# Hash attention and MLP on one core: the preparation of the first batch, and the order of the third chunk, written anew

## The chip, the core and the metric

The kernel runs on one core of a Trainium2 chip. The metric is the device time of one execution in microseconds (us). The kernel before was timed in three runs: 324.23, 325.96 and 326.18 us, median 325.96. All times below are from one profiled execution, counted from its first instruction.

## What is computed

```python
q_bits = (np.einsum('bhsd,dk->bhsk', q, proj) > 0)      # k_bits likewise; 6 bits
mask = q_bucket[:, :, :, None] == k_bucket[:, :, None, :]
scores = np.where(mask, scale * np.matmul(q, k.transpose(0, 1, 3, 2)), -1e9)
attn = softmax(scores); x = attn @ v                    # (4, 8, 768, 64)
# x as (4, 768, 512):
xn = (x - mu) / np.sqrt(var + 1e-06) * g_ln
out = x + np.maximum(xn @ w_ch1, 0.0) @ w_ch2           # 512 -> 2048 -> 512
```

There are 4 batches of 8 heads, with 768 tokens of 64 elements. A key counts for a query only when all six signs of their projections agree.

## The kernel before

**Trick of the mask.** The kernel puts the six sign bits beside the 64 elements of each query and key, as plus or minus one half or a multiple of it. One matmul over 70 rows then gives the score plus a large amount for equal bits; a bias in the exponential takes that amount off again, so that unequal hashes vanish. The operands stand in `slots`: rows 0 to 63 are the elements, rows 64 to 69 the bits, for each head, for queries and keys, with 768 columns in two halves (`par` 0 and 1).

**Chunks and units.** A chunk is 256 queries of one batch (`TT` = 2 tiles of 128), so each batch has three chunks, 12 in all. A chunk has 12 units (`att_units`, L385): three for each of four pairs of heads. A unit is 4 score matmuls (L403) into a tile `sc` in PSUM, one exponential on ScalarE (`ex`, L409, 128 x 1024) and 8 matmuls with the values (`av`, L437). At the third unit of a pair VectorE divides by the row sums (L452, L462). The first group of a pair needs head a alone; the second needs both heads. Behind attention comes the MLP of the chunk (`mlp_steps`, L470): norm, `xtrans`, eight `up` steps (8 matmuls L519 each, evacuated by `evac`, L125, to `hbuf`) and eight `down` steps (4 matmuls L536 each), which are spread as fillers between the units of the next chunk by `interleave` (L598) according to a cost written beside each step.

**Preparation of batch 0** is done by TensorE, since nothing else has run yet. For each head, `transposes` (L202) turns q and k with three transposes each into a PSUM tile `tpose` (VectorE evacuates q, L219, ScalarE k, L221, to `qkT` in f32), and `casts` (L223) writes `qkT` as bf16 into `slots`, one cast for each half. For each pair, `hash_pair` (L299) projects q (a = 0) and k (a = 1) with 4 matmuls each (L306), VectorE makes bits of them (L311), and four copies (L326, L324 or L322) of 6 x 768 put the bits into `slots`: two or three on VectorE, one on GpSimd, one on ScalarE for the first pair. `values` (L328) casts half of v for the matmuls with the values, `row_sums` (L349) prepares the row `vrows` with which every `av` begins in batch 0.

**The first two chunks** are one stage, `first_two` (L644), in an order written by hand (`tc.manual_schedule()`: each engine takes its instructions in the order of the program). The units go pair by pair, and the third chunk's first scores are the last of the list. In round i the scores of the next unit are issued, then the steps of `also[i]`, then the values of unit i. `keep_awake` issues matmuls on zeros. Loads: q, k and v of batch 0 on SP's queue (k of the first two heads and proj on ScalarE's), w1, w2 and batch 1 on GpSimd's.

**Preparation of batches 1 to 3** is named by letters in `plan` (L708): L load of q and k, W load of v, N narrowing cast on GpSimd (L239), T the DMA transpose into `slots` (L261) and the copy of half of it (L266), K and B block transposes on VectorE (L244), H hashes on TensorE (L275) with a way over DRAM for the bits (L288, L290), V cast and sums of values, E their share (L344), Q the squares on ScalarE (L191) for a safety test. These are fillers too. From the third chunk on, a scheduler may move instructions; it works with costs of its own.

**Buffers that matter:** `ps_sc`, `ps_av` and `ps_mm` have two tiles each; `tpose` (but for head 1), hashes, `rows`, `xnTp`, `hp` and `o2` share `ps_mm`. `qkT` has four, `nat16` one, `ex` three.

Of the kernel before, what the change touches and what calls it, by code (L numbers as in the profile page):

```python
# [28 lines left out]
def kernel(  # L29
# [12 lines left out]
    P = 128  # L42
# [115 lines left out]
    def load_values(b, half):  # L158
        h0 = half * H // 2
        eng = nc.gpsimd if (b, half) == (1, 0) else nc.sync  # L160
        if (b, half) == (0, 1):
# [6 lines left out]
        eng.dma_start(  # L168
            out=t, in_=v[b, h0 : h0 + H // 2].rearrange("h (p c) d -> p h c d", p=P)
        )  # L170
        return t

    class Prep:
# [28 lines left out]
        def transposes(self, h, a):  # L202
# [3 lines left out]
            if h == 1:  # L206
                tp = ps_sc.tile([P, 2, 512], F32, tag="sc", name="tpose")[:, 0, 0:HS]
# [10 lines left out]
            if a == 0:  # L218
                nc.vector.tensor_scalar_mul(self.qkT[h][:, a, :], tp, Q_SCALE)  # L219
            else:  # L220
                nc.scalar.activation(self.qkT[h][:, a, :], tp, AF.Copy)  # L221

        def casts(self, h):  # L223
            src = self.qkT[h]
            if h < 2:
                nc.gpsimd.tensor_copy(self.tokens(h, 0), src[0:D])
                nc.scalar.activation(self.tokens(h, 1), src[D:P], AF.Copy)
            else:
                eng = nc.gpsimd if h in (4, 6) else nc.vector
                eng.tensor_copy(self.tokens(h, 0), src[0:D])  # L230
                nc.vector.tensor_copy(self.tokens(h, 1), src[D:P])  # L231
# [67 lines left out]
        def hash_pair(self, j, a):  # L299
# [15 lines left out]
            if a == 0:  # L315
                return
            for g in range(4):
                par = g % 2
                dst = self.sl[D:K1, 2 * j + g // 2, :, par * HS : (par + 1) * HS]
                src = bits[32 * g : 32 * g + n_bits]  # L320
                if g == 2 and j == 0:
                    nc.scalar.activation(dst, src, AF.Copy)  # L322
                elif g == 3:
                    nc.gpsimd.tensor_copy(dst, src)  # L324
                else:
                    nc.vector.tensor_copy(dst, src)  # L326
# [143 lines left out]
    def mlp_steps(b, t, x):  # L470
# [41 lines left out]
        def up(n2):  # L512
# [3 lines left out]
            for i in range(2):  # L516
# [11 lines left out]
                scalar=b == 0 and t == 0 and n2 < NH // 2 - 2,  # L528
# [110 lines left out]
    def head(h):  # L639
        prep.transposes(h, 0)  # L640
        prep.transposes(h, 1)
        prep.casts(h)

    def first_two():  # L644
# [20 lines left out]
        keep_awake(10)  # L665
        prep.values(0)
# [5 lines left out]
            0: [lambda: head(2), lambda: prep.values(1)],  # L672
            1: [lambda: prep.row_sums(0), lambda: head(3), lambda: nxt.load(0)],
            3: [lambda: prep.hash_pair(1, 0)],
            4: [lambda: prep.hash_pair(1, 1)],
            5: [lambda: head(4), load_w2],
            6: [lambda: head(5)],
            7: [lambda: prep.hash_pair(2, 0)],
            8: [
                lambda: prep.row_sums(1), lambda: prep.hash_pair(2, 1), lambda: nxt.load(1), lambda: nxt.load_v(0),  # L680
            ],
            9: [lambda: head(6)],
            10: [lambda: head(7)],
            11: [lambda: prep.hash_pair(3, 0)],
            12: [
                lambda: prep.hash_pair(3, 1), lambda: nxt.narrow(0, 0), lambda: nxt.narrow(0, 1),
            ],
            14: [lambda: nxt.blocks(0, 0, 0)],
            15: [
                lambda: nxt.blocks(0, 0, 1),  # L690
            ],
# [12 lines left out]

# [31 lines left out]
    for n in range(2, len(chunks)):  # L736
# [4 lines left out]
        fillers = (mlp[0][1][1:] if n == 2 else []) + [norm]  # L741
        fillers += mixed(early, tail[:4]) + ([(600, xtrans)] if n == 2 else [])
        held = ups[-2:] if n == len(chunks) - 1 else []
        fillers += mixed(late, tail[4:]) + ups[: len(ups) - len(held)]
# [8 lines left out]
        interleave(units[n], fillers, after, begun=True)  # L753
# [190 lines left out]
```

## Time and profile before

| what | value |
|---|---|
| three runs | 324.23, 325.96, 326.18 us; median 325.96 us |
| profiled execution | span 325.2 us from first to last instruction; a time of its own around that span is not given |
| TensorE matmul busy | 305.4 us (94%), 3249 instructions |
| ScalarE, VectorE, GpSimd busy | 216.8, 181.4, 83.8 us |
| exponentials | 144 of 1114 ns, 159.7 us |
| up matmuls, down matmuls | 99.0 us, 92.4 us |
| first exponential; first of the third chunk | 11.99 us; 52.06 us |

A matmul's busy time is partly modelled, so that a busy TensorE is not one at its peak. "Granted clock" (PEclk) is the share of the TensorE clock that its throttle let through. In tables of waits, an engine and line stand ahead of the arrow and what ended the wait behind it, then total, times, and the longest, in us. Lines of the timeline have the start, the length, engine, line, operation, output <- input, and in brackets the idle time before it and what ended it.

### The profile page before, as it was taken

Reading aid. Unit: us, or ns where it says so; the run is one execution under the profiler, and the core shown is the slowest. Engines: PE = TensorE matmul, PEld = TensorE weight load, DVE = VectorE, ACT = ScalarE, POOL = GpSimd, SP = SyncE. Lnnn points to the kernel's source line nnn. Section 1 sums busy time; section 2 is a strip of 40 time slices with the busy share of each in tenths; the row PEclk is TensorE's granted clock in tenths of the full one; section 3 lists DMA queues with packets and bytes.
Section 4 is the critical chain, followed back from the end, with each engine's and each line's share of the span. In section 5 each row is a group of like instructions: output and inputs, shape, how many; then the busy total and the mean of one; then the engine's idle time right before and its main releaser. Section 6 shows DMA issues by size and latency. Waiting matters only on the chain.

```text
span 325.2 us, 7843 instructions
## 1 busy us (share of the span) xinstructions
PE 305.4 (94%) x3249; PEld 225.9 (69%) x3276; DVE 181.4 (56%) x399; ACT 216.8 (67%) x274; POOL 83.8 (26%) x105
## 2 busy tenths in 40 slices
PE   6888899999999999999999999989999999999991
PEld 5655568767758868858768769759679688685750
DVE  1578974483575695446596674534643735446320
ACT  4567687935685886876976866997667568672110
POOL 4546623744032260056082040200200200201000
PEclk9999967999999999999999999999999999999998
DMA  7999996985289469497444552030020200200201
GB/s 225 366 211 301 208 331 110 214 250 135 63 187 262 109 166 204 90 266 241 80 111 85 71 120 50 1 89 12 19 80 2 65 34 2 65 34 15 87 27 46
DMA packets 64875, 40.94 MB, mean 126 GB/s; under 512 B 47184, under 2 KB 59728, under 8 KB 64832
## 3 DMA queue, kind: packets, MB, share of 16 engines
q1 hardware_dynamic: 60368, 31.85, 39.2%
q0 software_dynamic: 4096, 8.13, 10.5%
q8 instruction: 27, 0.44, 0.6%
q10 hardware_dynamic: 368, 0.39, 0.4%
q14 instruction: 16, 0.13, 0.1%
HBM read 27.98 MB, written 6.88 MB: 107 GB/s over the span
## 4 chain that ended last, share of the span: by engine, by line
PE 81%; ACT 9%; DVE 5%; issue 3%; ACTq 0%; DVEq 0%
PE hp L519 25%; PE o L536 21%; PE sc L403 17%; PE av L437 10%; ACT ex L409 4%; PE hash L275 3%; DVE slots L326 2%; PE hash L306 2%; ACT qnat L191 1%; ACT knat L191 1%; PE tpose L211 1%; PE wakep L656 1%; DVE bits L311 1%; ACT hbuf L133 1%; DVE slots L231 1%
## 5 line engine op out<-in xcount | busy, mean ns | idle before, releaser
L409 ACT ACTIVATE ex<-sc,expb 128x1024 bf16<-128x1024 f32 x144 | 159.7, 1114 | 65.7 <-PE sc L403 65.0
L519 PE MATMUL hp<-xnT,w_sb 128*128 128x256 bf16 x768 | 99.0, 273 | 0.3 <-ACT hbuf L133 0.3
L536 PE MATMUL o<-w_sb,hbuf 128*128 128x512 bf16 x357 | 92.4, 379 | 1.9 <-ACT hbuf L133 0.7
L403 PE MATMUL sc<-slots 70*128 70x256 bf16 x576 | 90.0, 278 | 3.3 <-DVE slots L326 2.9
L519 PEld LDWEIGHTS <-w_sb 128*128 128x128 bf16 x768 | 72.4, 98 | 9.6 <-issue 0.6
L437 PEld LDWEIGHTS <-ex 128*128 128x128 bf16 x1152 | 54.4, 99 | 22.6 <-ACT ex L409 9.3
L403 PEld LDWEIGHTS <-slots 70*128 70x128 bf16 x576 | 52.1, 99 | 17.5 <-DVE slots L326 2.7
L437 PE MATMUL av<-vaug,ex 128*128 128x65 bf16 x1152 | 60.8, 196 | 2.6 <-ACT ex L409 2.4
L129 DVE TENSOR_SCALAR hbuf<-hp 128x512 bf16<-128x512 f32 x45 | 31.0, 688 | 49.2 <-PE hp L519 48.4
L536 PEld LDWEIGHTS <-hbuf 128*128 128x128 bf16 x384 | 35.5, 97 | 29.2 <-issue 1.2
L497 POOL TENSOR_SCALAR rs<-mv 128x2 f32<-128x2 f32 x12 | 6.2, 513 | 168.0 <-DVE mv L482 167.9
L133 ACT ACTIVATE hbuf<-hp 128x512 bf16<-128x512 f32 x51 | 30.4, 596 | 21.6 <-PE hp L519 21.4
L541 DVE SCALAR_TENSOR_TENSOR x<-o,rs,x 128x512 f32<-128x512 f32 x24 | 17.8, 741 | 33.3 <-PE o L536 33.3
L462 DVE TENSOR_TENSOR x<-x,rc 128x256 f32<-128x256 f32 x36 | 20.7, 574 | 1.0
L454 DVE TENSOR_SCALAR rc<-av 128x4 f32<-128x4 f32 x36 | 5.7, 158 | 23.6 <-PE av L437 23.6
L483 DVE SCALAR_TENSOR_TENSOR xn<-x,mv,gbc 128x512 bf16<-128x512 f32 x24 | 18.0, 766 | 0.1
L481 DVE BATCH_NORM_STATS2 stats<-x 128x6 f32<-128x512 f32 x24 | 15.4, 678 | 0.2
L330 POOL CAST vaug<-vnat 128x1536 bf16<-128x1536 f32 x8 | 12.2, 1525 | 10.5 <-DMA vnat<-in_v_dram 5.5
L455 DVE TENSOR_TENSOR x<-av,vsum 128x256 f32<-128x256 f32 x36 | 14.9, 413 | 0.0
L191 ACT ACTIVATE knat<-knat 128x768 f32<-128x768 f32 x16 | 13.5, 848 | 0.0
L191 ACT ACTIVATE qnat<-qnat 128x768 f32<-128x768 f32 x16 | 13.5, 844 | 0.0
L239 POOL CAST nat<-qnat 128x1536 bf16<-128x1536 f32 x6 | 9.0, 1501 | 16.7 <-DMA qnat<-in_q_dram 10.7
(79 smaller groups left out, 207.6 us busy)
## 6 DMA issues: line engine op xcount, KB each, us to landing
out_dram<-x SPq DMA_DIRECT2D x24, 256.0 KB
vnat<-in_v_dram SPq DMA_DIRECT2D x7, 768.0 KB
qnat<-in_q_dram SPq DMA_DIRECT2D x11, 384.0 KB
knat<-in_k_dram SPq DMA_DIRECT2D x11, 384.0 KB
w_sb<-in_moe_w_ch_dram POOLq DMA_DIRECT2D x4, 1024.0 KB, 13.7
slots<-slots SPq DMA_DIRECT2D x6, 384.0 KB
qnat<-in_q_dram POOLq DMA_DIRECT2D x2, 768.0 KB, 13.3
knat<-in_k_dram POOLq DMA_DIRECT2D x2, 768.0 KB, 14.6
```

Of the source, the lines that this page charges most:

```text
L129: nc.vector.tensor_scalar_max(dst, src, 0.0)
L133: nc.scalar.activation(dst, src, AF.Relu if relu else AF.Copy)
L191: nc.scalar.activation(src, src, AF.Square, accum_out=sq[:, a, col : col + 1],)
L403: nc.tensor.matmul(sc[:, i, :], sl[0:K1, h, 1, kj * P : (kj + 1) * P], sl[0:K1, h, 0, q0 : q0 + CT],)
L409: nc.scalar.activation(ex, sc, AF.Exp, bias=expb[:, 1:2] if b else expb[:, 0:1], scale=scale if b else scale / Q_SCALE,)
L437: nc.tensor.matmul(av[:, h - ha, qi, :], state[g][:, i, qi * P : (qi + 1) * P], va[:, h, CMAP[b][kj], :], start=(b > 0 and (g, i, qi) == ( ...
L462: nc.vector.tensor_tensor(xv, num, rc.unsqueeze(3).to_broadcast([P, 2, TT, D]), op=AOP.mult)
L481: nc.vector.bn_stats(stats, x[:, i, :])
L483: nc.vector.scalar_tensor_tensor(xn[:, :, i, :], x[:, i, :].rearrange("p (o d) -> p o d", d=P), mv[:, i, 0:1], gbc.rearrange("p (o d) -> p ...
L519: nc.tensor.matmul(hp[:, i, :], w1_sb[:, dt, nt * P : (nt + 1) * P], st["xnT"][:, dt, :], start=(dt == 0), stop=(dt == ND - 1),)
L536: nc.tensor.matmul(o2, st["h"][:, nt, i * P : (i + 1) * P], w2_sb[:, nt, :], start=(nt == 0), stop=(nt == NH - 1),)
L541: nc.vector.scalar_tensor_tensor(x[:, i, :], o2, st["rs"][:, i : i + 1], x[:, i, :], op0=AOP.mult, op1=AOP.add,)
```

## The change

In the first stage:

- `casts` becomes `cast(h, par, eng)`, for one half at a time, with the engine named. Heads 0 and 1 are cast by VectorE, ScalarE, GpSimd and ScalarE; heads 2 to 7 by VectorE alone (before, GpSimd had one half of heads 0, 1, 4 and 6).
- The bit copies become `bit_rows(j)`, all four on VectorE for every pair.
- The transposes of heads 2 and 3 come ahead of the first scores, behind the first hash; those of head 2 go into a tile of `ps_sc` and are evacuated by ScalarE alone, those of head 3 take both tiles of `ps_av`. Heads 4 and 5 are turned in rounds 4 and 5 (before 5 and 6), heads 6 and 7 still in rounds 9 and 10; each pair's casts follow two rounds or one later. Pair 1's hash is one round earlier.
- Two of the three `keep_awake` calls (3 and 10 matmuls) are left out.
- proj is loaded on SP's queue behind the first head of q. The first half of batch 0 of v is loaded in two pieces, the first ahead of heads 2 and 3 of q and k, and cast in two pieces (`pair_values`).
- The narrowing casts and block transposes of batch 1 come one round later.

For the third chunk the order is written by hand and kept (`manual_schedule`), with the same steps in another order: the second hash of batch 1 and the four squares come near its end, and the loads of batch 2 wait for these squares. All eight `up` steps of the first chunk are evacuated by VectorE and ScalarE in turn (before, the first six by ScalarE).

```diff
+            if (b, half, hi) == (0, 0, 1):
+                nc.sync.dma_start(out=proj1[0:D, 0, 0:n_bits], in_=proj)
+            if (b, half, hi) == (0, 0, 2):
+                t["v"] = load_values(b, half, 0, 2)
         if b == 0 and half == 0:
-            nc.scalar.dma_start(out=proj1[0:D, 0, 0:n_bits], in_=proj)
             nc.scalar.activation(wake2[:, 0:1], wake2[:, 1:2], AF.Exp)
-            t["v"] = load_values(b, half)
+            load_values(b, half, 2, 4, t["v"])
...
+    def copy_by(eng, dst, src):
+        if eng == "A":
+            nc.scalar.activation(dst, src, AF.Copy)
+        else:
+            (nc.vector if eng == "V" else nc.gpsimd).tensor_copy(dst, src)
...
+        def transposes(self, h, a, space="mm", eng=None):
...
+            if space == "sc":
+                if a == 0:
+                    self.tp2 = ps_sc.tile([P, 2, 512], F32, tag="sc", name="tpose")
+                tp = self.tp2[:, a, 0:HS]
+            elif space == "av":
+                tp = ps_av.tile([P, HS], F32, tag="av", name="tpose")
...
-        def casts(self, h):
...
+        def cast(self, h, par, eng):
+            copy_by(eng, self.tokens(h, par), self.qkT[h][par * D : (par + 1) * D])
...
+        def bit_rows(self, j, engs="VVVV"):
             for g in range(4):
...
+                copy_by(engs[g], dst, self.pair_bits[32 * g : 32 * g + n_bits])
+        def pair_values(self, j):
+            hs = slice(2 * j, 2 * j + 2)
+            nc.gpsimd.tensor_copy(self.va[:, hs, :, 0:D], self.tiles[j // 2]["v"][:, 2 * (j % 2) : 2 * (j % 2) + 2])
...
-                scalar=b == 0 and t == 0 and n2 < NH // 2 - 2,
...
+        T, C, B = prep.transposes, prep.cast, prep.bit_rows
         keep_awake(26)
-        head(0)
-        head(1)
+        T(0, 0)
+        T(0, 1)
+        T(1, 0, "sc")
+        T(1, 1, "sc")
+        C(0, 0, "V")
+        C(0, 1, "A")
+        C(1, 0, "G")
+        C(1, 1, "A")
         nc.vector.tensor_copy(proj1[D : 2 * D, 1, 0:n_bits], proj1[0:D, 0, 0:n_bits])
-        keep_awake(3)
+        prep.pair_values(0)
         prep.hash_pair(0, 0)
         prep.hash_pair(0, 1)
-        keep_awake(10)
-        prep.values(0)
+        T(2, 0, "sc", "A")
+        T(2, 1, "sc", "A")
+        B(0)
+        T(3, 0, "av", "V")
+        T(3, 1, "av", "A")
+        prep.pair_values(1)
         load_w1()
...
         also = {
+            0: [lambda: C(2, 0, "V"), lambda: C(2, 1, "V")],
+            1: [lambda: C(3, 0, "V"), lambda: C(3, 1, "V"), lambda: prep.row_sums(0)],
+            2: [lambda: prep.hash_pair(1, 0), lambda: prep.values(1)],
+            3: [lambda: prep.hash_pair(1, 1), lambda: B(1), lambda: nxt.load(0)],
+            4: [lambda: T(4, 0), lambda: T(4, 1)],
+            5: [lambda: T(5, 0), lambda: T(5, 1), lambda: load_w2()],
+            6: [lambda: C(4, 0, "V"), lambda: C(4, 1, "V")],
+            7: [lambda: C(5, 0, "V"), lambda: C(5, 1, "V"), lambda: prep.hash_pair(2, 0)],
+            8: [lambda: prep.hash_pair(2, 1), lambda: B(2), lambda: prep.row_sums(1), lambda: nxt.load(1), lambda: nxt.load_v(0)],
+            9: [lambda: T(6, 0), lambda: T(6, 1)],
+            10: [lambda: T(7, 0), lambda: T(7, 1), lambda: C(6, 0, "V"), lambda: C(6, 1, "V")],
+            11: [lambda: C(7, 0, "V"), lambda: C(7, 1, "V"), lambda: prep.hash_pair(3, 0)],
+            12: [lambda: prep.hash_pair(3, 1), lambda: B(3)],
+            13: [lambda: nxt.narrow(0, 0), lambda: nxt.narrow(0, 1)],
+            15: [lambda: nxt.blocks(0, 0, 0)],
+            16: [lambda: nxt.blocks(0, 0, 1)],
...
+        if n == 2:
+            u0, d0 = mlp[0][1], mlp[0][2]
+            pr = prepare
+            fillers = u0[1:3] + pr("K10")[:1] + u0[3:5] + pr("K10")[1:] + pr("N11") + u0[5:8]
+            fillers += [norm] + d0[:2] + pr("H10") + pr("V10 W11") + pr("B11")[:2] + d0[2:4]
+            fillers += pr("T11") + [(600, xtrans)] + pr("B11")[2:] + d0[4:8] + ups[:4]
+            fillers += pr("E10 Q00 L20") + ups[4:6] + pr("H11") + ups[6:] + pr("V11 W20")
...
+        with ExitStack() as fixed:
+            if n < 3:
+                fixed.enter_context(tc.manual_schedule())
+            interleave(units[n], fillers, after, begun=True)
```

More of the change, by code (lines that the diff above doesn't have):

```diff
@@ L150, in load_half, with load_values @@
                 )
+            if (b, half, hi) == (0, 0, 1):
+                nc.sync.dma_start(out=proj1[0:D, 0, 0:n_bits], in_=proj)
+            if (b, half, hi) == (0, 0, 2):
+                t["v"] = load_values(b, half, 0, 2)
         if b == 0 and half == 0:
-            nc.scalar.dma_start(out=proj1[0:D, 0, 0:n_bits], in_=proj)
             nc.scalar.activation(wake2[:, 0:1], wake2[:, 1:2], AF.Exp)
-            t["v"] = load_values(b, half)
+            load_values(b, half, 2, 4, t["v"])
         return t
-    def load_values(b, half):
+    def load_values(b, half, lo=0, hi=None, t=None):
+        hi = H // 2 if hi is None else hi
         h0 = half * H // 2
         eng = nc.gpsimd if (b, half) == (1, 0) else nc.sync
-        if (b, half) == (0, 1):
+        if t is not None:
+            pass
+        elif (b, half) == (0, 1):
             t = work.tile([P, NH * CT // 2], F32, tag="h", bufs=1, name="vnat1")[
@@ L314, in hash_pair @@
             )
-            if a == 0:
-                return
+        def bit_rows(self, j, engs="VVVV"):
             for g in range(4):
@@ L637 @@
     mlp = {0: mlp_steps(*chunks[0], xs[0])}
[L639 to L642, printed above, removed]
     def first_two():
@@ L740 @@
         early, late = (prepare(part) for part in (plan.get(n, "") + "|").split("|")[:2])
-        fillers = (mlp[0][1][1:] if n == 2 else []) + [norm]
-        fillers += mixed(early, tail[:4]) + ([(600, xtrans)] if n == 2 else [])
         held = ups[-2:] if n == len(chunks) - 1 else []
-        fillers += mixed(late, tail[4:]) + ups[: len(ups) - len(held)]
+        if n == 2:
[5 more added lines that the diff above has]
+            fillers += pr("E10 Q00 L20") + ups[4:6] + pr("H11") + ups[6:] + pr("V11 W20")
+        else:
+            fillers = [norm] + mixed(early, tail[:4])
+            fillers += mixed(late, tail[4:]) + ups[: len(ups) - len(held)]
         tail = held + downs
```

52 lines of the change are left out of this document (9 added, 43 removed).

## The prediction

> **What bounds the kernel now.** I read the page's slices first, then the work by stretch, TensorE's waits, and the timeline of VectorE and ScalarE where TensorE waits.
>
> ```profile
> PE   6888899999999999999999999989999999999991
> PEclk9999967999999999999999999999999999999998
> ```
>
> TensorE is full from the seventh slice (about 49 us) on; only the first six have gaps, and there the clock is also low once. By stretch (columns: length, then TensorE, weight loads, VectorE, ScalarE, GpSimd busy, then granted clock, DMA share, GB/s):
>
> ```profile
> 10.00:20.00 10.00, 8.79 (x104) 6.14 (x101) 6.49 (x12) 7.65 (x10) 6.44 (x7) 1.00 1.11 305
> 20.00:30.00 10.00, 8.62 (x107) 5.68 (x100) 7.69 (x16) 6.31 (x9) 4.78 (x6) 1.00 1.08 267
> 30.00:42.50 12.50, 9.87 (x126) 6.16 (x125) 11.36 (x20) 9.56 (x11) 8.01 (x8) 1.00 1.20 240
> 42.50:52.50 10.00, 9.92 (x86) 7.53 (x87) 5.07 (x11) 7.05 (x7) 1.50 (x2) 0.50 1.10 270
> 52.50:90.00 37.50, 36.69 (x408) 27.94 (x411) 21.37 (x41) 24.98 (x37) 16.69 (x18) 1.00 0.61 151
> ```
>
> Ahead of 42.5 TensorE idles 1.21 + 1.38 + 2.63 us; behind 52.5 it has 0.81 us to give in 37.5. So the change can earn only in the first stage. What TensorE waits for there:
>
> ```profile
> PE sc L403 <- DVE slots L326: 2.9, 6, 0.7
> PE hash L306 <- ACT slots L227: 1.9, 1, 1.9
> PE tpose L211 <- DVE qkT L219: 0.8, 1, 0.8
> ```
>
> The largest wait is for VectorE's copies of the bits. These take 351 ns alone, and far longer beside GpSimd:
>
> ```profile
> L326 DVE COPY slots<-bits x11: 351/644/1504, 10.3 to 38.3; 6x768 bf16<-6x768 bf16 x11
> ...
> 17.67 1.85 DVE L231 CAST slots<-qkT 64x768 bf16<-64x768 f32 x1
> 36.99 2.79 DVE L326 COPY slots<-bits 6x768 bf16<-6x768 bf16 x3
> ...
> 17.64 1.47 POOL L330 CAST vaug<-vnat 128x1536 bf16<-128x1536 f32 x1 [3.02 <-DMA vnat<-in_v_dram]
> 37.02 1.01 POOL L324 COPY slots<-bits 6x768 bf16<-6x768 bf16 x1 [2.99 <-DVE bits L311]
> ```
>
> The cast at 17.67 takes 1.85 us where its like at 17.10 took 0.55: it stood still for GpSimd's 1.47 us. The three copies at 36.99 cost 2.79 us instead of 3 x 0.35. Of 11 copies the mean is 7.58 / 11 = 0.69 us.
>
> **The change, part by part.** I walk the first stage by the exponentials (1.11 us each), whose starts mark the units. A unit costs TensorE 0.68 us at full clock (values to scores 0.24, scores to values 0.44, as at 16.38, 16.62 and 17.06), a hash 0.78, a head's transposes 0.66.
>
> Start. The hash stood from 6.1 to 7.97 for proj, whose DMA was third on ScalarE's queue (issued 1.67, VectorE's copy of it 7.93). It moves to second on SP's queue, ahead of q's second head; that head and half of v move behind it. Half of v is 0.39 MB, about 1 us at the 380 GB/s of these microseconds, so heads 2 and 3 arrive at about 8.5 instead of 7: just in time for their new place behind the first hash. The hash starts when VectorE has done evacuation, cast and proj copy, 6.22 + 0.56 + 0.17 = 6.95; 1 us is gained. The 13 dropped wake matmuls (0.33 + 0.72 us) lay in waits: nothing. Bits end at 9.2. Then four copies on VectorE instead of two there, one on ScalarE, one on GpSimd: 4 x 0.35 alone, 2.6 us with a value cast of 0.75 beside them. Transposes of heads 2 and 3 (1.3 us) stand ahead of the first scores, under those copies. First exponential about 11.3, between 10.75 and 12.0, against 11.99.
>
> Pair 1. Head 3's transposes now hold both value banks of PSUM, so unit 0's values wait for its evacuation, which is behind the four copies: 12.4. Units 3 to 5 then need no evacuation on ScalarE. The hash of pair 1 runs in iterations 2 and 3 instead of 3 and 4; its copies start near 18.1, beside the second cast of values and GpSimd's DMA issues (0.77 each), so 0.7 to 0.8 each. Head 4's evacuation stands behind them and head 5's transposes need its bank. Unit 6's exponential at 20.4 (before 22.72), unit 7's at 23.5 (before 24.10): most of the lead is spent on this new wait.
>
> Pairs 2 and 3. GpSimd loses two casts (1.21, 1.08) and three bit copies (0.94, 1.01, 1.01) here and runs through its DMA issues by 25, so the VectorE copies should mostly take 0.35 to 0.4. VectorE gains one copy per pair and two casts (0.55 each). Unit 10 at 28.2 (29.87), unit 12 at 31.2 (34.07). Before unit 15 the last four copies end between 36.1 (GpSimd idle) and 37.8 (both narrowing casts of 1.47 beside them); TensorE waits about 1.7 us for them. Unit 16's exponential lands between 37.3 and 39.3 against 40.31: -1.0 to -3.0. My walk leaves out small handshakes, so I take -1.9, nearest the middle. GpSimd issues the same bytes earlier, but the 16 engines are over 1.0 busy until 49, so the later landings hardly move.
>
> Units 16 to the end of the stage. Work is unchanged: scores, values, exponentials, the norm, xtrans, the first up. In the profile this went at half clock:
>
> ```profile
> 44.37 2.30 ACT L409 ACTIVATE ex<-sc,expb 128x1024 bf16<-128x1024 f32 x2 [0.82 <-PE sc L403]
> 47.11 1.11 ACT L409 ACTIVATE ex<-sc,expb 128x1024 bf16<-128x1024 f32 x1 [0.44 <-PE sc L403]
> 48.41 1.11 ACT L409 ACTIVATE ex<-sc,expb 128x1024 bf16<-128x1024 f32 x1 [0.18 <-PE sc L403]
> 52.06 1.11 ACT L409 ACTIVATE ex<-sc,expb 128x1024 bf16<-128x1024 f32 x1 [1.03 <-PE sc L403]
> ```
>
> Units 18 to 23 came every 1.49 us (42.45 to 49.91). At full clock ScalarE would set 1.13: 5 x 0.36 = 1.8, and with the slower xtrans and first up 2.9 us. The fall came in a stretch of nothing but scores and values, behind short waits (0.70, 0.47). The new order keeps such a stretch, with a longer wait in it: I take the same fall, 0; its end would be worth -2.9. The Trainium skill (TensorE: Matmul & The Clock Gate, Why this matters for your kernels) says that the clock falls where TensorE idles for some 3 us between bursts; here it fell with no gap above 0.70, so the trace disagrees; by that rule the new kernel, which has no such gap either, would not fall.
>
> Third chunk. Chunk 0's ups alternate between VectorE and ScalarE instead of six on ScalarE: the wait of 0.27 at 56.3 goes, -0.3. The four squares move from four places (53.9 to 60.2) into one run behind up 3, 4 x 0.82 = 3.3 us on ScalarE; behind them stand the evacuation of up 5 and unit 11's exponential. TensorE has about 4.3 us of work in hand (two ups, scores, a hash, values), then waits 0 to 1.5, say 0.8. The second hash of batch 1 moves from 70.6 to about 82; its bounce through DRAM (72.2 to 82.8 in the trace) still ends some 6 us before unit 6 of the next chunk. Sum +0.5. From the fourth chunk on the order on TensorE is the same: 0.
>
> Sum: -1.9 + 0 + 0.5 = -1.4. On the profiled execution, whose span is 325.2 (what lies around it is not shown; the median of the runs is 325.96, 0.76 more), that is 323.8 of span, and 325.96 - 1.4 = 324.6 us for a run. A rule of the Trainium skill bears on the copies: SBUF — State Buffer, Who interferes with whom, says that a VectorE copy or cast in a two-port mode and a GpSimd instruction exclude each other for a whole instruction. The cast of 1.85 beside 1.47 agrees.
>
> **The rivals.**
> One, the clock does not fall: waits at pair 3 shorter than I think, or the hp matmuls come in time. For it: waits of 1.7 us at 20.7 and 31.4 did not lower the clock. Against: those lay among hashes and transposes. 324.6 - 2.9 = 321.7. The rule of the Trainium skill cited above (TensorE: Matmul & The Clock Gate) leads here too.
>
> Two, slower: VectorE becomes the bound of the first stage. From the first copies (9.25) to the last it has 16 copies of c, 12 casts (6.7), 5 evacuations (2.8), 6 bits (3.2), 4 divisions (2.4): 15.1 + 16c, and about 3 us in which it must wait. Unit 16 comes 1 us behind that. At c = 0.75 that is 9.25 + 27.1 + 3 + 1 = 40.3, no gain; at c = 1.0 it is 44.4, 4.1 late, 325.96 + 4.1 + 0.5 = 330.6. For it: copies beside GpSimd reached 1.50. Against: most of the GpSimd work that stretched them is taken away, and the mean with it was 0.69.
>
> Three, the fixed third chunk stalls at its end. The loads of batch 2 wait for the squares, so they move from 63 to 68 to about 81 to 85 and land near 87 (four of 384 KB, 1 us each at 380 GB/s), where VectorE's block transposes (88.49 in the trace) stand in its queue ahead of the norm. If they land 2.5 us late TensorE loses that much: 327.1.
>
> Four, nothing is gained: the half of v ahead of heads 2 and 3 delays the start by 1 us and pair 1's new wait eats the rest: 326.0.
>
> **How the numbers follow.** Forecast 0.45 (own range 323.2 to 326.0), clock does not fall 0.23, VectorE bounds 0.15, end of chunk three 0.10, nothing gained 0.07. One per cent, 3.26 us, is about what a measurement of this kernel can tell from no change. Below 322.7 lies nearly all of rival one: faster 0.24. Above 329.2 lies most of rival two and a deep case of three: slower 0.17. The same 0.59. The range 321.0 to 328.6 leaves out most of rival two and the edge of rival one, together some 0.19.
>
> **What would show it.** Right: hash at about 7, the bit copies near 0.35 to 0.45 behind 25 us, unit 16's exponential near 38.4, scores still waiting for copies at pairs 1 and 3, clock 0.50 for some 7 to 10 us behind 38, a short gap behind the four squares. Wrong: copies at 0.7 or more throughout, a clock of 1.00 up to 50 (rival one), or TensorE gaps behind 52 above 2 us (rival three).

## The result, and the profile after

The changed kernel takes 337.41 us (median of 4 runs, 336.56 to 338.05); the kernel before took 326.07 us on the same chip (4 runs, 324.23 to 326.43). The ratio is 1.0381, 95% interval 1.0328 to 1.0434: slower by 3.8%, where 324.6 us was forecast. Each ratio, here and in the table of runs below, is against the kernel before timed beside it on the same chip and leaves out executions more than 1.5% above the fastest of their kernel (five of twelve in e8), while the medians are of all. The profiled execution took 336.88 us, its span is 335.1 us, so 1.8 us lie around the span.

The two lines of the page that show TensorE's busy tenths and its granted clock by slices (8.4 us each):

```profile
PE   6989899999981999999999999989999999999991
PEclk9899758999996799999999999999999999999998
```

There is a hole in the thirteenth slice (about 100 to 109 us), where the kernel before had none, and a low clock in it and right behind it. The starts of the exponentials put a length on it. The third chunk begins at 52.04 us (before 52.06) and the fourth at 84.86 (85.11); the fifth begins at 120.66 (110.57); from there to the last exponential both kernels take 182 us. So the loss of this execution, 10.3 us, lies in the fourth chunk: 35.8 us instead of 25.5. In these two profiles the first stage came out even, and the third chunk took 32.8 us instead of 33.0.

TensorE's waits from 60 to 130 us, first in the kernel before (all of them), then in the changed one (the largest; no other is above 0.8 us):

```profile
PE av L437 <- ACT ex L409: 0.3, 1, 0.3
```

```profile
PE hp L531 <- DMA xnT<-xn: 7.1, 1, 7.1
```

One wait of 7.1 us for one transfer is most of the loss. `xnT` is the transposed norm of the third chunk, made by a DMA transpose that SP issues; the eight `up` steps need it. Then comes the price of the gap itself. By stretch, with the columns of the prediction (length; TensorE, weight loads, VectorE, ScalarE, GpSimd busy; granted clock, DMA share, GB/s), changed kernel:

```profile
84.86:96.00 11.14, 10.41 (x97) 6.58 (x96) 8.02 (x15) 9.21 (x16) 2.65 (x2) 1.00 0.64 191
96.00:108.00 12.00, 4.66 (x63) 2.91 (x64) 3.94 (x12) 3.26 (x3) 2.62 (x4) 0.80 0.92 197
108.00:114.00 6.00, 5.57 (x41) 4.30 (x42) 0.69 (x1) 1.71 (x2) 0.00 (x0) 0.54 1.08 254
114.00:121.00 7.00, 7.00 (x84) 6.33 (x82) 3.08 (x7) 4.63 (x6) 4.24 (x4) 1.00 0.53 134
```

From 108 to 114 us the clock is 0.54: 5.57 us of TensorE work that full speed does in some 3. So 7.1 + 2.6 of the 10.3 us are the wait and the low clock behind it. The Trainium skill (TensorE: Matmul & The Clock Gate, Why this matters for your kernels) says that an idle gap of about 3 us costs the clock; behind these 7.11 us the trace agrees.

Why xnT came late is read from SP's own queue. First the kernel before, then the changed one (start, length of the issue, line, operation, output <- input):

```profile
75.27 0.50 SPq L288 DMA_DIRECT2D bits_d<-bits  x1
...
78.42 0.39 SPq L168 DMA_DIRECT2D vnat<-in_v_dram  x1
78.91 3.92 SPq L290 DMA_DIRECT2D slots<-bits_d  x4
...
89.81 4.36 SPq L261 DMA_TRANSPOSE slots<-nat  x1
94.27 1.23 SPq L492 DMA_TRANSPOSE xnT<-xn  x1
```

```profile
83.88 1.56 SPq L147 DMA_DIRECT2D qnat<-in_q_dram  x1
...
86.93 0.46 SPq L147 DMA_DIRECT2D knat<-in_k_dram  x1
87.49 0.41 SPq L301 DMA_DIRECT2D bits_d<-bits  x1
94.50 3.04 SPq L303 DMA_DIRECT2D slots<-bits_d  x4
97.64 0.45 SPq L173 DMA_DIRECT2D vnat<-in_v_dram  x1
...
98.77 6.39 SPq L274 DMA_TRANSPOSE slots<-nat  x1
105.25 1.26 SPq L504 DMA_TRANSPOSE xnT<-xn  x1
```

The input of xnT was ready at about the same time in both: VectorE's last norm operation ended at 91.8 us after the change and about 91 before. But SP takes its issues one by one. The second bounce of batch 1's bits (`bits_d`, then `slots<-bits_d`) starts 12 us later than before, takes 6.95 us to land, four loads of batch 2 having just been issued ahead of it, and SP stands until 94.5 waiting for it. Behind it stands the load of v for batch 2, then batch 2's first DMA transpose, and behind that xnT, issued at 105.25 instead of 94.27. The trace's chain of waits has these links among others:

```profile
87.49 6.95 DMA bits_d<-bits
...
103.47 1.48 POOL vaug L342
104.95 0.20 SPq L274
...
105.25 3.13 DMA xnT<-xn
```

One of these links does not hold. The chain says that the transpose at L274 waited for GpSimd's cast of v, which ended at 104.95. But what it reads is `nat`, whose last cast had ended at 96.22, and in other runs its issue ended well behind the cast of v: 103.33 and 101.42 in e4, 102.80 and 99.91 in e13. More likely the traffic on the DMA engines drew the issue out: it took 6.39 us at a busy share of 1.07 (the transpose's own bytes included), against 3.71 us at 0.78 in e3. No run tried that by itself.

The answers to the prediction's other views. The first stage by stretch, changed kernel:

```profile
10.00:20.00 10.00, 9.34 (x100) 5.40 (x91) 6.90 (x15) 7.61 (x10) 4.58 (x5) 0.95 1.11 314
20.00:30.00 10.00, 8.79 (x115) 6.41 (x111) 8.96 (x20) 7.24 (x10) 5.93 (x8) 1.00 1.10 284
30.00:42.50 12.50, 10.93 (x128) 6.86 (x126) 10.15 (x20) 9.32 (x11) 3.28 (x2) 0.83 1.21 226
42.50:52.50 10.00, 9.73 (x87) 7.52 (x85) 5.08 (x11) 6.91 (x7) 1.49 (x2) 0.52 1.14 241
```

TensorE's wait for VectorE's copies there, 2.9 us before, and these copies, four for each pair:

```profile
PE sc L415 <- DVE slots L183: 1.5, 1, 1.5
```

```profile
11.92 1.90 DVE L183 COPY slots<-bits 6x768 bf16<-6x768 bf16 x4
20.47 1.82 DVE L183 COPY slots<-bits 6x768 bf16<-6x768 bf16 x4
28.41 1.45 DVE L183 COPY slots<-bits 6x768 bf16<-6x768 bf16 x4
37.18 1.49 DVE L183 COPY slots<-bits 6x768 bf16<-6x768 bf16 x4
```

These are 6.66 us for 16 copies, 0.42 each (0.37 behind 25 us), where 11 copies had a mean of 0.69 before. The copies did what the change says.

### The profile page after: what moved, and what is told of

It is laid out like the page before. It is cut to its first block, busy times and chain, and to the rows that moved or that the text cites. A ratio compares the mean times of both kernels' runs of the same rounds, so it can differ in the third digit from the quotient of the medians.

```text
span 335.1 us, 7800 instructions
## 1 busy us (share of the span) xinstructions
PE 308.5 (92%) x3236; PEld 226.5 (68%) x3263; DVE 183.0 (55%) x409; ACT 215.2 (64%) x271; POOL 77.1 (23%) x99
## 4 chain that ended last, share of the span: by engine, by line
PE 76%; DVE 7%; DMA 6%; ACT 4%; issue 2%; SPq 1%; POOL 0%; ACTq 0%; DVEq 0%
PE hp L531 25%; PE o L547 19%; PE sc L415 17%; PE av L449 10%; DVE slots L183 3%; PE hash L288 2%; DMA bits_d<-bits 2%; ACT ex L421 2%; DMA vnat<-in_v_dram 2%; DMA qnat<-in_q_dram 1%; PE hash L319 1%; ACT knat L203 1%; DMA xnT<-xn 1%; DVE bits L324 1%; SPq L303 1%
## 5 line engine op out<-in xcount | busy, mean ns | idle before, releaser
L531 PE MATMUL hp<-xnT,w_sb 128*128 128x256 bf16 x768 | 100.3, 276 | 7.3 <-DMA xnT<-xn 7.1
L415 PE MATMUL sc<-slots 70*128 70x256 bf16 x576 | 91.0, 282 | 1.9 <-DVE slots L183 1.5
L449 PEld LDWEIGHTS <-ex 128*128 128x128 bf16 x1152 | 55.2, 100 | 22.7 <-ACT ex L421 9.2
L129 DVE TENSOR_SCALAR hbuf<-hp 128x512 bf16<-128x512 f32 x48 | 33.1, 689 | 59.6 <-PE hp L531 58.8
L449 PE MATMUL av<-vaug,ex 128*128 128x65 bf16 x1152 | 61.6, 197 | 2.2 <-ACT ex L421 2.2
L415 PEld LDWEIGHTS <-slots 70*128 70x128 bf16 x576 | 52.9, 100 | 15.3 <-DVE slots L183 2.0
L133 ACT ACTIVATE hbuf<-hp 128x512 bf16<-128x512 f32 x48 | 28.5, 593 | 22.2 <-PE hp L531 22.2
L552 DVE SCALAR_TENSOR_TENSOR x<-o,rs,x 128x512 f32<-128x512 f32 x24 | 17.7, 740 | 32.2 <-PE o L547 32.2
L474 DVE TENSOR_TENSOR x<-x,rc 128x256 f32<-128x256 f32 x36 | 19.4, 539 | 1.0
L252 POOL CAST nat<-qnat 128x1536 bf16<-128x1536 f32 x6 | 9.0, 1499 | 33.0 <-DMA qnat<-in_q_dram 25.5
L342 POOL CAST vaug<-vnat 128x1536 bf16<-128x1536 f32 x7 | 10.3, 1467 | 22.3 <-DMA vnat<-in_v_dram 17.5
```

The costliest lines, as they stand in the source:

```text
L129: nc.vector.tensor_scalar_max(dst, src, 0.0)
L133: nc.scalar.activation(dst, src, AF.Relu if relu else AF.Copy)
L415: nc.tensor.matmul(sc[:, i, :], sl[0:K1, h, 1, kj * P : (kj + 1) * P], sl[0:K1, h, 0, q0 : q0 + CT],)
L449: nc.tensor.matmul(av[:, h - ha, qi, :], state[g][:, i, qi * P : (qi + 1) * P], va[:, h, CMAP[b][kj], :], start=(b > 0 and (g, i, qi) == ( ...
L474: nc.vector.tensor_tensor(xv, num, rc.unsqueeze(3).to_broadcast([P, 2, TT, D]), op=AOP.mult)
L531: nc.tensor.matmul(hp[:, i, :], w1_sb[:, dt, nt * P : (nt + 1) * P], st["xnT"][:, dt, :], start=(dt == 0), stop=(dt == ND - 1),)
```

## The experiments

Two theories stood after the result. Theory A: xnT stands in SP's queue behind the late bounce and behind the transpose that waits for late data; the order of that queue is the loss. Theory B: the loads of batch 2, late because the squares are late, cost by themselves. The table has all runs; "third" and "fourth" are the time from a chunk's first exponential to the next chunk's, from the profile of each run, and "xnT" TensorE's wait for it.

| run | median, us | ratio to before, 95% interval | third | fourth | xnT |
|---|---|---|---|---|---|
| before | 326.07 | | 33.0 | 25.5 | 0 |
| changed | 337.41 | 1.0381 (1.0328 to 1.0434) | 32.8 | 35.8 | 7.1 |
| e1_old_third | 331.27 | 1.0134 (1.0079 to 1.0189) | 37.9 | 25.5 | 0 |
| e2_new_third | 333.97 | 1.0256 (1.0185 to 1.0327) | 32.7 | 35.3 | 6.8 |
| e3_hash_first | 335.63 | 1.0292 (1.0208 to 1.0376) | 34.8 | 31.8 | 1.7 |
| e4_loads_early | 336.89 | 1.0346 (1.0299 to 1.0393) | 32.8 | 36.6 | 7.6 |
| e5_both_early | 327.67 | 1.0111 (1.0026 to 1.0196) | 32.9 | 26.6 | 0.9 |
| e6_old_third_evac | 327.34 | 1.0053 (1.0001 to 1.0104) | 33.8 | 25.5 | 0 |
| e7_xnT_act | 345.43 | 1.0627 (1.0544 to 1.0711) | 33.0 | 44.0 | (see text) |
| e8_q_first | 327.87 | 1.0016 (0.9964 to 1.0069) | 33.8 | 25.5 | 0 |
| e9_wake | 328.58 | 1.0127 (1.0045 to 1.0209) | 33.5 | 30.1 | 2.5 |
| e10_fourth_fixed | 334.10 | 1.0266 (1.0203 to 1.0328) | 33.0 | 32.4 | 3.4 |
| e11_before_wake | 323.41 | 0.9927 (0.9903 to 0.9950) | 32.9 | 25.5 | 0 |
| e12_first_wake | 323.97 | 0.9912 (0.9877 to 0.9946) | 32.9 | 25.5 | 0 |
| e13_hash_first_fourth | 333.99 | 1.0275 (1.0184 to 1.0367) | 35.1 | 30.4 | 0 |

**Which part of the change.** e1 keeps the new first stage and takes the third chunk back to the old list and the scheduler; the `up` steps are still evacuated in turn.

```diff
-            fillers += pr("E10 Q00 L20") + ups[4:6] + pr("H11") + ups[6:] + pr("V11 W20")
...
+        fillers = (mlp[0][1][1:] if n == 2 else []) + [norm]
...
-            if n < 3:
-                fixed.enter_context(tc.manual_schedule())
```

> The new first stage with the third chunk as it was before (its list of steps and the scheduler's freedom). If the loss lies in the third chunk's order, this runs like the kernel before, since the third chunk's first exponential starts at 52.04 in the changed kernel and at 52.06 before: 326 us, between 324.5 and 327.5. If the new first stage costs time further on, or the two only hurt together, it is 329 or more.

e2 is the other half: the kernel before with the new list and fixed order of the third chunk, the first stage untouched.

> The kernel before with the new third chunk alone (new list of steps, order kept). If the third chunk's order is the whole loss: 336 to 338, with a wait of some 7 us of the fourth chunk's first up for xnT. If the loss needs the new first stage too: under 330.

The fourth chunk is back at 25.5 us in e1 and lost 9.8 us in e2, with the same wait (6.8 us). So the new third chunk makes that wait, with the old first stage too. It is most of the loss and not shown to be all of it: e2 took 333.97 us, short of the 336 to 338 forecast, and its ratio is below the changed kernel's. e1 took 331.27, in the range of its second case: its third chunk takes 4.8 us longer than before. TensorE waits there for evacuations:

```profile
PE hp L531 <- DVE hbuf L129: 2.0, 1, 2.0
PE hp L531 <- ACT hbuf L133: 1.5, 1, 1.5
```

e6 settles that: it is e1 with the old rule for chunk 0's evacuations put back.

```diff
                 st["h"][:, 2 * n2 : 2 * n2 + 2, :], hp, relu=True,
+                scalar=b == 0 and t == 0 and n2 < NH // 2 - 2,
```

> The earlier run with the new first stage and the old third chunk, now also with the old rule that ScalarE evacuates the first six ups. That run waited 3.5 us for evacuations in its third chunk, with a fall of the clock behind it. If the evacuation in turn does that (VectorE has the norm and block transposes ahead of its share), the third chunk takes 33 us again (37.9 there) and the run is 324.5 to 327.5. If the first stage does it by its late DMA transpose, 329 to 332 again.

The third chunk falls from 37.9 to 33.8 and the time from 331.27 to 327.34. So evacuating in turn costs 4 us with the old order. What is left, the new first stage alone, is 1.0053 (1.0001 to 1.0104): no gain. Its third chunk is still 0.8 us longer than before; TensorE waits 1.9 us there for one evacuation by ScalarE.

**Which step of the third chunk.** e3 moves the second hash (H11, with its bounce) ahead of squares and loads, which stay late.

```diff
-            fillers += pr("E10 Q00 L20") + ups[4:6] + pr("H11") + ups[6:] + pr("V11 W20")
+            fillers += pr("E10 H11") + pr("Q00 L20") + ups[4:6] + ups[6:] + pr("V11 W20")
```

> The changed kernel, in the third chunk the second hash of batch 1 moved ahead of the four squares and of the loads of batch 2; these stay late. If the late hash with its way over DRAM is what stops SP's queue, the wait for xnT goes: 326 to 328. If the late loads of batch 2 stop it (the narrowing cast, the DMA transpose and xnT's transpose all stand behind them), the wait stays at 5 us or more: 333 to 338.

e4 does the opposite: squares and loads early, the hash late.

> The changed kernel, in the third chunk the four squares and the loads of batch 2 moved ahead of the first hash; the second hash stays late. If the late loads are the cause: 326 to 328, wait for xnT under 1 us. If the late hash alone is enough to stop SP's queue: 331 or more.

e5 moves T11, H11, the squares and the loads early.

```diff
-            fillers += [norm] + d0[:2] + pr("H10") + pr("V10 W11") + pr("B11")[:2] + d0[2:4]
-            fillers += pr("T11") + [(600, xtrans)] + pr("B11")[2:] + d0[4:8] + ups[:4]
-            fillers += pr("E10 Q00 L20") + ups[4:6] + pr("H11") + ups[6:] + pr("V11 W20")
+            fillers += [norm] + d0[:2] + pr("T11") + pr("H10") + pr("V10 W11") + pr("B11")[:2] + d0[2:4]
+            fillers += [(600, xtrans)] + pr("B11")[2:] + d0[4:6] + pr("H11 Q00 L20") + d0[6:8] + ups[:4]
+            fillers += pr("E10") + ups[4:8] + pr("V11 W20")
```

> The changed kernel with, in the third chunk, the second DMA transpose, the second hash and the squares with the loads of batch 2 all early (ahead of the last two downs of chunk 0). If SP's queue, held up by either of the two late steps, is the loss, the fourth chunk takes 25.5 us between its first exponential and the next chunk's (35.8 in the changed kernel) and the run 324.5 to 327.5. If the new first stage or the fixed order costs something else, 329 or more.

One alone does not bring the time back. The third and fourth chunks together take 58.5 us before, 68.6 in the changed kernel, 66.6 in e3, 69.4 in e4 and 59.4 in e5. e3 came out between its two cases (the time of the second, a wait for xnT of 1.7 us), e4 as its second case has it; e5 took 327.67 us, just above its range. Since e5 moves T11 too, it does not show that the other two steps are enough without it. SP's queue in e4 and then in e5:

```profile
86.12 1.60 SPq L301 DMA_DIRECT2D bits_d<-bits  x1
91.65 3.03 SPq L303 DMA_DIRECT2D slots<-bits_d  x4
94.73 0.50 SPq L173 DMA_DIRECT2D vnat<-in_v_dram  x1
...
95.89 7.44 SPq L274 DMA_TRANSPOSE slots<-nat  x1
103.42 1.25 SPq L504 DMA_TRANSPOSE xnT<-xn  x1
```

```profile
73.72 0.33 SPq L301 DMA_DIRECT2D bits_d<-bits  x1
...
84.39 0.41 SPq L173 DMA_DIRECT2D vnat<-in_v_dram  x1
...
91.94 3.99 SPq L274 DMA_TRANSPOSE slots<-nat  x1
96.03 1.23 SPq L504 DMA_TRANSPOSE xnT<-xn  x1
```

With the bounce late, v and the transpose are late whatever the loads do. With the bounce early (e3), the loads of batch 2 stand behind it and go out from 88.89 us on, 5 us later than in the changed kernel. The same transpose then waits for the cast of these loads: it went out at 98.66 and xnT at 102.48. VectorE waits for them as well, with a block transpose ahead of the norm, and TensorE behind VectorE; first VectorE's line, then TensorE's wait in e3:

```profile
92.53 0.98 DVE L257 STREAM_TRANSPOSE bt<-qnat 128x768 f32<-128x768 f32 x1 [6.56 <-DMA qnat<-in_q_dram]
```

```profile
PE o L547 <- DVE vsum L357: 2.4, 1, 2.4
```

**Past the queue.** e7 gives the third chunk's xnT to ScalarE's queue.

```diff
-                nc.sync.dma_start_transpose(
+                (nc.scalar if (b, t) == (0, 2) else nc.sync).dma_start_transpose(
```

> The changed kernel, with the DMA transpose xnT of the third chunk issued from ScalarE's queue instead of SP's; nothing else. If its place in SP's queue makes it late (xn is ready near 91.8, issued at 105.3), the wait of 7.1 us shrinks to 2 or less and the run is 326 to 330. If the DMA engines are simply full then, the wait stays at 5 or more: 334 to 338.

This run, at 345.43 us, lies outside both forecasts and separates neither theory. The issue on ScalarE still waited for batch 2's first DMA transpose on SP's queue, which landed at 106.7 us; ScalarE's exponentials waited 17.0 us behind it, and TensorE stood 17.4 us for them. It shows only that an engine with work of its own was a bad place for this issue.

e10 reaches the same end in another way: the fourth chunk's order too is kept as written, and so xnT stands ahead of batch 2's transpose.

```diff
-            if n < 3:
+            if n < 4:
                 fixed.enter_context(tc.manual_schedule())
```

> The changed kernel, with the fourth chunk's order also kept as the program writes it. Nothing else differs: the second bounce of the hash bits is as late as before (about 87). Theory, the order of SP's queue: xnT's transpose is then issued ahead of batch 2's first DMA transpose in the queue and no longer waits behind a transpose that waits for the late loads; TensorE's wait of 7.1 us for xnT in the fourth chunk falls to 1 us or less, the chunk's first exponential to the next chunk's takes 26 to 28 us instead of 35.8, and the time is 326 to 330 us. Rival, the late data: the loads of batch 2 and what is made from them are late by themselves, so that the fourth chunk waits 4 us or more for something else, and the time stays at 333 us or more.

The wait fell to 3.4 us and the fourth chunk to 32.4, between the two forecasts; the time, 334.10 us, is in the rival's range. SP's queue of e10:

```profile
87.02 0.41 SPq L301 DMA_DIRECT2D bits_d<-bits  x1
93.71 3.05 SPq L303 DMA_DIRECT2D slots<-bits_d  x4
96.86 0.45 SPq L173 DMA_DIRECT2D vnat<-in_v_dram  x1
97.42 1.29 SPq L504 DMA_TRANSPOSE xnT<-xn  x1
```

xnT is issued 7.8 us earlier than in the changed kernel, right behind the bounce and the 768 KB of v, and TensorE goes on at 103.92, 6.5 us after the issue instead of 3.2. The bounce still holds the issue. That the landing is late because v's bytes are ahead of it on the DMA engines is likely, but no run tried it.

e13 takes both out of xnT's way, the hash early (as e3) and the fourth chunk fixed (as e10). The loads are not as late as in the changed kernel, as the forecast has it, but later: they start at 89.03 us, behind the bounce, instead of 83.88.

> The changed kernel with the second hash of batch 1 ahead of the squares and loads, and with the fourth chunk's order kept as the program writes it; the loads of batch 2 stay late. So xnT's transpose stands in SP's queue behind neither the late bounce of the bits nor batch 2's first DMA transpose. Theory, the two together hold xnT back: TensorE's wait for xnT in the fourth chunk is 1 us or less, the chunk takes 26 to 28 us from its first exponential to the next chunk's, and the time is 326 to 330 us, though the loads of batch 2 are as late as in the changed kernel. Rival, the late loads cost by themselves, by their bytes on the DMA engines or by VectorE's work on them: the fourth chunk still waits 3 us or more, in all, and the time is 332 us or more.

TensorE's largest wait in the fourth chunk of e13, then VectorE's block transposes:

```profile
PE hash L288 <- DVE x L552: 3.8, 1, 3.8
```

```profile
92.87 0.98 DVE L257 STREAM_TRANSPOSE bt<-qnat 128x768 f32<-128x768 f32 x1 [4.50 <-DMA qnat<-in_q_dram]
...
96.10 1.80 DVE L257 STREAM_TRANSPOSE bt<-knat 128x768 f32<-128x768 f32 x2
```

The wait for xnT is gone, so Theory A's mechanism is right: the order of SP's queue made it. But the fourth chunk still takes 30.4 us and the run 333.99, no less than e10, because a hash now waits 3.85 us. The trace puts the end of that wait to VectorE's sum at L552, which stands in VectorE's queue behind the block transposes, the hash's own input; and these waited 4.50 us and then 1.35 us more for the late loads. So late loads do cost by themselves, as Theory B says, as the next gate behind the first. What they cost at their place in the changed kernel e13 does not show: there the same hash waited 0.79 us. Of the runs tried, only e5, with both steps early, gave most of the time back (1.0111 instead of 1.0381).

**The clock.** Six matmuls on zeros are added to each of rounds 13 to 21 of the first stage: e9 adds them to e5, e11 to the kernel before.

```diff
+        for i in range(13, 22):
+            also.setdefault(i, []).insert(0, lambda: keep_awake(6))
```

> The run with both steps early, and six matmuls on zeros in each of rounds 13 to 21 of the first stage, in TensorE's wait for the exponential. If the clock falls there because scores and values alone are too little work, it stays at 1.00 and the run is some 2.9 us under the one without them: 321 to 324.5. If these matmuls do not count, or cost as much as they save: within 1 us of it.

> The kernel before, with six matmuls on zeros added to each of rounds 13 to 21 of the first stage, and nothing else. Theory, the clock's fall is a loss of its own: the granted clock is 1.00 up to 52 us, the third chunk's first exponential comes near 49.2 instead of 52.06, and since xnT of the fourth chunk had some 3.5 us of slack on SP's queue here, the gain stays: 322 to 324 us. Rival, it is given back as in the run with both bounces early: the third or fourth chunk waits for the transposes on SP's queue, whose time is set by the DMA engines, and the time is 325 to 327 us.

The stretch that the prediction showed at clock 0.50, in e11:

```profile
42.50:52.50 10.00, 9.78 (x145) 8.74 (x143) 6.90 (x15) 9.64 (x11) 1.50 (x2) 1.00 1.17 256
```

In both the clock is 1.00 from 7 us to the end of the third chunk. In e11 the third chunk begins at 49.23 us instead of 52.06, and the run takes 0.9927 (0.9903 to 0.9950) of the time before. The kernel before shows the same price by itself: of its 28 executions beside e11, four had a mean granted clock of 0.994 to 0.996 and took 323.03 to 324.12 us, the others had 0.974 to 0.980 and took 325.59 us or more; all twelve of e11 had 0.991 or more and took 322.88 to 324.40. In e9 the third chunk begins 3.4 us earlier than in e5 and nothing is won, because xnT leaves SP's queue at 96.39 as in e5 (96.03): TensorE waits 2.5 us for it. A lead ahead of a queue that does not move is no lead.

**The start.** e8 is e6 with proj's DMA behind q of the second head.

```diff
-            if (b, half, hi) == (0, 0, 1):
+            if (b, half, hi) == (0, 0, 2):
                 nc.sync.dma_start(out=proj1[0:D, 0, 0:n_bits], in_=proj)
-            if (b, half, hi) == (0, 0, 2):
                 t["v"] = load_values(b, half, 0, 2)
```

> The new first stage with the old third chunk and its old evacuation, and with the small DMA of proj issued behind q of the second head instead of ahead of it. Theory, proj's DMA of 64 rows of 24 bytes held q of the second head back: TensorE's transposes of head 1 start near 5.1 instead of 6.4, its idle stretch ahead of the first hash shrinks, the granted clock does not fall there, and the first exponential comes at 11.3 instead of 12.0 to 14.1; the time is 0.5 to 1.5 us below the 327.3 of the same kernel with proj ahead. Rival, half of v and the DMA engines delay that head anyway, or proj becomes the last to arrive: first exponential at 12 or later, time as before, 327.

e12 adds the matmuls on zeros to e8.

> The same kernel with proj behind q of the second head, and with six matmuls on zeros in each of rounds 13 to 21 too. Theory, the new first stage is worth something once the clock holds: the third chunk's first exponential comes at 46 to 48 and the time is 321 to 324 us, below both kernels. Rival, SP's queue and the DMA engines set the third chunk's work: the lead is given back as waits for batch 1's data or for xnT, and the time is 325 to 327 us, no better than the kernel before with the same matmuls added.

The start came out as e8's theory says. TensorE in the changed kernel, in e6, which differs from e8 in proj's place alone, and in e8:

```profile
6.47 0.55 PE L227 MATMUL tpose<-identf,qnat 128*128 128x128 f32 x3 [1.54 <-DMA qnat<-in_q_dram]
...
8.51 2.74 PE L319 MATMUL hash<-qkT,proj 128*32 128x384 f32 x16
```

```profile
5.86 0.55 PE L227 MATMUL tpose<-identf,qnat 128*128 128x128 f32 x3 [0.44 <-DMA qnat<-in_q_dram]
...
7.54 1.67 PE L319 MATMUL hash<-qkT,proj 128*32 128x384 f32 x16
```

```profile
5.12 0.50 PE L226 MATMUL tpose<-identf,qnat 128*128 128x128 f32 x3
...
6.74 1.67 PE L318 MATMUL hash<-qkT,proj 128*32 128x384 f32 x16
```

The hash starts 0.8 us earlier than in e6 and 1.8 us earlier than in the changed kernel, whose clock had fallen there, and the first exponential comes at 11.22 us (12.02 and 14.06). The time does not follow beyond doubt: 1.0016 (0.9964 to 1.0069) against e6's 1.0053 (1.0001 to 1.0104), and the median of all, 327.87 us, is not below e6's. In e12 the third chunk begins at 49.49 us, not at the forecast 46 to 48; in its profile the clock fell at 22 us, ahead of the added matmuls. Its ratio, 0.9912, is no better than that of e11, 0.9927, which has the old first stage: their intervals overlap. Both beat the kernel before and the changed one. Yet the three executions of e12 with the highest clock (0.993 to 0.995) took 320.80 to 322.67 us, less than any of e11's twelve, so the new first stage may be worth a microsecond or two where the clock holds throughout. Three executions do not show it.

## Why the prediction was wrong, step by step

**The step that failed** is the last of the sum: "From the fourth chunk on the order on TensorE is the same: 0." It measured +10.3 us in the profile: 7.1 of waiting for xnT, some 2.6 of low clock behind it, and little else. The order on TensorE was the same; the order and the times on SP's queue were not. The working had looked at the data that the second hash delivers: its bounce "still ends some 6 us before unit 6 of the next chunk". That deadline was kept, but barely: the last of the bits' issues ended at 97.54 us and the scores of unit 6 began at 98.31. TensorE does not wait for the bits. But a bounce is two issues on an in-order queue with a wait between them, and behind it stand v, a DMA transpose and xnT. What is queued behind a moved instruction was worked out for ScalarE's squares and not for SP. xnT had a slack of about 3.4 us before (landed at 97.39, used at 100.76), and was issued 11 us later. e10 and e13 show that the order of SP's queue made the wait, e2 that the new third chunk brings it without the new first stage.

**Rival three** had the right place and the right cause for half of it: loads of batch 2 late behind the squares. It put the price at 2.5 us and the wait at VectorE's block transposes ahead of the norm. In the changed kernel VectorE did wait there (0.96 and 1.46 us, at 89.09 and 93.22), but the norm was ready at 91.8 all the same; the loads stood ahead of the bounce on SP's queue, and the bounce took 6.95 us to land behind them. The rival as written is seen in e3, where the loads are 5 us later still: VectorE's block transpose waits 6.56 us ahead of the norm, and TensorE 2.35 us behind it. In e13 the wait behind the block transposes is 3.85 us.

**Third chunk, +0.5:** measured -0.2 in the profile, a size within what one profile can tell. Of its parts, "-0.3" for evacuating in turn has no run that bears it out: with the old order the same edit costs 4 us (e1 against e6). Why the new order is spared was not tried.

**The copies** were right: 0.42 us each, and VectorE is not the bound (rival two). Its most loaded stretch, 20 to 30 us, is at 8.96 of 10.

**First stage, -1.9:** in the changed kernel's profile unit 16's exponential came at 39.44 instead of the forecast 38.4 (before 40.31), and the lead was gone at the third chunk: 52.04. The start was put at 11.3 and came at 14.06. The text expected heads 2 and 3 late behind v; instead q of head 1 was late, by proj's DMA ahead of it, as e8 shows. And "The 13 dropped wake matmuls (0.33 + 0.72 us) lay in waits: nothing" is left open: with them gone TensorE had only six transposes from 5 to 8.5 us, the clock fell to 0.50 and the hash took 2.74 us instead of 1.67. In the ten profiles with proj's DMA ahead of that load the hash took 2.6 to 2.8 us in four (the first exponential then at 13.9 to 15.0) and 1.67 in six (11.9 to 12.4). In three of the four the clock had fallen; in the fourth, e4, its record begins only at 13.0 us. In e8 and e12, with q early and the matmuls still gone, the hash took 1.67. No run puts the matmuls back with proj ahead, so their share is not shown. Of the late start a part was made good: unit 12 came at 32.70, where 31.2 was forecast and 34.07 was before. The late stretch at half clock, 38.4 to 52, ate the rest.

The changed kernel's profile was in part bad luck. In e3, e5 and e6, which have the same first stage, a first exponential at 12.0 to 12.4 and a clock that held until 39 us, unit 6 came at 20.4 to 20.6 (forecast 20.4), unit 12 at 31.1 to 31.4 (31.2), unit 16 at 38.1 to 39.1 (38.4) and the third chunk at 50.1 to 50.9. But the old first stage varies as well: with it the first exponential came at 11.99 and the third chunk at 52.06 in the kernel before, at 10.67 and 50.63 in e2. One profile each cannot tell a lead of 1.9 us from that.

**The clock fall, taken as 0,** was right for the changed kernel: it came again, and started 4 us before its place in the kernel before. That "its end would be worth -2.9" was right too: e11 is 2.8 us earlier at the third chunk and 0.7% faster.

**The other rivals.** The fourth, that nothing is gained in the first stage, is what e6 and e8 show: 1.0053 and 1.0016. Rival one leans on "waits of 1.7 us at 20.7 and 31.4" that did not lower the clock; the trace has no such waits there, but shorter ones, 0.72 and 0.40 us behind 20.7 and 0.20 and 0.78 us behind 31.2.

## What to carry to other kernels

When a step moves, walk every in-order queue that it issues on, not only its data's deadline: a DMA that waits for another DMA blocks all that stands behind it, and the instruction that suffers can belong to another batch. Where two late steps stand one behind the other, undoing one shows little, so an experiment must undo both before either is acquitted. And a gain ahead of a fixed transfer chain is worth only that chain's slack; measure the slack first.

## What the runs showed of the hardware

- The granted clock fell to 0.50 without a long idle gap. In nine of the twelve profiles without the added matmuls it fell to 0.50 somewhere between 35 and 53 us, in a stretch of scores and values with short waits; the longest idle gap of TensorE in the 8 us ahead of it was 0.70 us in the kernel before and at most 2.61 (e5). With 54 small matmuls added over nine rounds it stayed at 1.00 there in all three profiles. In the other three without them it stayed at 1.00 there as well: in two of them it had fallen between 24 and 32 us instead, in one (e4) it was 1.00 from 13.0 us, where its record begins, to 101.8. The added matmuls are no cure for the whole stage: in e12 the clock fell between 21 and 29 us, ahead of them. What sets the moment is open.
- The issue of a DMA transpose (L274, half a batch) held SP's queue for very different times, longest where the DMA engines were busiest: in the changed kernel 16.20 us at a busy share of 1.17 (from 34.71), 6.39 at 1.07, 3.67 at 0.86 (from 186.52 us). Between these the two do not go strictly together: 5.42 us at 0.99, 3.70 at 1.01 (from 73.28 and 162.63). The longest ended no earlier than in the kernel before, which issued it at 41.13 (9.28 us). Issuing it earlier gained nothing.
- A DMA of proj, 64 rows of 24 bytes, ahead of a load of 192 KB on the same queue moved TensorE's use of that load from 5.0 and 5.1 us (e12, e8) to between 5.8 and 6.6 us (ten profiles).
